# Loading tokens ten blocks ahead in smaller transfers, weights last, and a running maximum in four tiles: a gated long convolution with a soft mixture of experts

## The chip, the core and the metric

The program runs on one core of one Trainium2 chip. The metric is the device time of one execution in microseconds (us), lower is better. A core has a matrix engine (PE, with its weight loads shown apart as PEld), a vector engine (DVE), a scalar engine (ACT), GpSimd (POOL) and SyncE (SP), which here only issues transfers. Sixteen DMA engines carry all transfers.

## What is computed

Two stages follow each other. The first is a long convolution done with FFTs and gated by its input; the second is a soft mixture of experts over the 45,824 tokens of 128 features that come out of it.

```python
u = x * v                                   # batch 4, sequence 11456, 128 features
y = irfft(rfft(u, 2*S) * rfft(filter, 2*S))[:S]
x = (x * y).reshape(45824, 128)

logits = x @ phi                            # 32 slots = 8 experts x 4
d = softmax(logits, over tokens)            # dispatch
slot_input = d.T @ x
h = relu(slot_input[e] @ w1[e])             # 128 -> 1024, for each of 8 experts e
slot_out[e] = h @ w2[e]                     # 1024 -> 128
c = softmax(logits, over the 32 slots)      # combine
out = c @ slot_out
```

All arithmetic is float32.

## The kernel before

**Convolution.** It runs over eight groups of 16 features. A group's last step (`p4`) gives, for seven row blocks in the order 1, 2, 3, 4, 5, 6, 0, a tile of tokens that is gated (`p4_gate`, `last_gate`) and written to a scratch buffer `scr` in device memory (`p4_out`, L465; the remainder by `p4_rest`, L471). `scr` holds x with the 128 features as rows. The last group can only be written at the very end, so its 16 rows (`CG`) of x are the last to come.

**Mixture of experts.** The tokens are cut into 23 blocks of 16 x 128 tokens (the last has 6 x 128), 1 MB each, and two blocks make a unit. Each block is read back from `scr` by `Moe.load` (L692 to L701): one transfer for each part of `scr` that the block touches, up to 2048 tokens long. There are ten places for blocks: five in `ahead_buf` (the tile `ffw`, which is free early) and five in `xbuf` (four in the tile `xreg`, one in the tile `E`). Blocks 0 to 4 go to `ahead_buf`; their first 112 rows (features of groups 0 to 6) are loaded while the last group still computes (`weights`, L655), and their last 16 rows later, by `ahead(t)` (L722), which runs behind each of the seven row blocks t of the last group. Blocks 5 to 9 are loaded whole by `ahead`.

For each unit m the loop of `_moe` does, on PE in this order: `turn` of the unit's first block (32 transposes of 64 x 64, L714), `logits` of the next unit (L780), `turn` of the second block, `dispatch` of the unit before (64 products, L872, four tiles of 32 columns side by side), and `running_max` (L820): one full 128 x 128 product that spreads the row maxima to all partitions, read by a reduction on DVE (L821). The exponentials on ACT (L831) wait for that reduction, and the next unit's logits need the PSUM bank that those exponentials read. Each of these products is issued twice by the hardware's float32 scheme, so a `dispatch` is 64 MATMUL rows and a `running_max` two.

Behind the turn of block i, `fetch(i)` (L952) refills the place that has come free: blocks 10 to 19 behind turns 0 to 9; the eight w1 matrices, two behind each of turns 10 to 13 (`load_w1`, into `ffw`); three w2 matrices behind turn 14; blocks 20 to 22 behind turns 15 to 17; the other five w2 matrices behind turns 18 to 20. One of the three w2 matrices has a place of its own in `ffw`, and the scheduler issues it early. After the last unit come the experts (`up`, `turn_hidden`, `down`) and then the output stage (`spread`, L1128 and L1136), in which 23 MB are written.

**Order of the transfers.** SP issues all of them in program order and stops at one that has to wait. The framework gives them eight completion semaphores in turn, so a transfer also waits until the one eight places before it has landed: at most eight are under way.

Of the kernel before, what the change touches and what calls it, by code (L numbers as in the profile page):

```python
# [29 lines left out]
CG = D // G  # L30
# [33 lines left out]
def conv_part(ctx, tc, cp, moe, xf, vf, xi, xe, pos, w1, w2, win, t1x, t1h, wt, t3, t4, hs, scr):  # L64
# [418 lines left out]
    for g in range(G + 1):  # L483
# [50 lines left out]
        else:  # L534
# [9 lines left out]
            for u in range(NU):  # L544
                p3(g - 1, u)
            moe.places()
            moe.steps = _moe(moe)
            next(moe.steps)

# [89 lines left out]
class Moe:  # L639
# [4 lines left out]
    OB = 4  # L644
    CB = 8 * NB

    def __init__(self, tc, cp, scr, phi, mw1, mw2, rep, out):
# [4 lines left out]
        self.xt, self.xq = {}, {}  # L652
        self.pieces = sorted(_pieces().values())

    def weights(self):  # L655
        nc = self.tc.nc
        w = self.cp.tile([128, 11 * FF], F32, tag="W", name="ffw")
        self.w1t = w[:, : 8 * FF].rearrange("p (e f) -> p e f", e=NEXP)
        self.w2t = {e: w[:, (8 + e) * FF : (9 + e) * FF].rearrange("p (j d) -> p j d", d=128)
                    for e in range(3)}  # L660
# [9 lines left out]
    def load_w1(self, e):  # L670
        self.tc.nc.sync.dma_start(out=self.w1t[:, e], in_=self.mw1[e])

    def load_w2(self, e):
        self.tc.nc.sync.dma_start(out=self.w2t[e],
                                  in_=self.mw2[e])

# [15 lines left out]
    def load(self, i, d0=0, d1=D):  # L692
        q0, n = self.blocks[i]
        t = (self.ahead_buf if i // self.XB in (0, 2) else self.xbuf)[i % self.XB][:, : 128 * n]
        z0, z1 = 128 * q0, 128 * (q0 + n)
        for a, m in self.pieces:
            lo, hi = max(z0, a), min(z1, a + B * m)
            if lo < hi:
                src = self.scr[D * a : D * (a + B * m)].rearrange("(d t) -> d t", d=D)
                self.tc.nc.sync.dma_start(out=t[d0:d1, lo - z0 : hi - z0], in_=src[d0:d1, lo - a : hi - a])  # L700
        self.xt[i] = t.rearrange("p (q t) -> p q t", t=128)  # L701
# [20 lines left out]
    def ahead(self, t):  # L722

        if t == 0:
            make_identity(self.tc.nc, self.ident)
            self.tc.keep_in_program_order(self.tc.nc.vector.tensor_reduce(
                out=self.mask, in_=self.ident.rearrange("p (a s) -> p a s", a=4), axis=AX.X, op=ALU.add))
        for i in ((), (0, 1), (2, 3, 4, 5), (6, 7), (8,), (9,), ())[t]:
            self.load(i, D - CG if i < self.XB else 0)


def _moe(mo):
# [5 lines left out]
    ident = mo.ident  # L738
    phis, reps, w1t, w2t = mo.phis, mo.reps, mo.w1t, mo.w2t

# [206 lines left out]
    hT = mo.obuf[OB - 1].rearrange("p (e j a s) -> p e j a s", e=2, j=FF // 128, a=4)  # L947
    def load_w2(e, j):
        w2t[e] = mo.xbuf[j % XB].rearrange("p (h j d) -> p h j d", h=2, d=128)[:, (e - 3) % 2]
        mo.load_w2(e)  # L950

    def fetch(i):  # L952
        if i < 2 * XB:
            mo.load(i + 2 * XB)
        elif i < 2 * XB + 4:
            for e in range(2 * (i - 2 * XB), 2 * (i - 2 * XB) + 2):
                mo.load_w1(e)
        elif i < 3 * XB:
            for e in range(3):
                mo.load_w2(e)  # L960
# [106 lines left out]
    def up(eg, hf):  # L1067
        ph = mo.plp.tile([128, 512], F32, tag="pl", name=f"ph_{eg}_{hf}")
        for a in range(4):
            inorder(nc.tensor.matmul(ph[32 * a : 32 * a + 32, :], lhsT=siT,  # L1070
                                     rhs=w1t[:, 4 * eg + a, 512 * hf : 512 * hf + 512],
                                     start=True, stop=True, tile_position=(0, 32 * a)))
# [12 lines left out]
    def down(eg, j0=0, j1=FJ):  # L1085
        for j in range(j0, j1):
            for a in range(4):
                inorder(nc.tensor.matmul(po[32 * a : 32 * a + 32, :], lhsT=hT[:, eg, j, a, :],  # L1088
                                         rhs=w2t[4 * eg + a][:, j, :], start=(eg == 0 and j == 0),
                                         stop=(eg == 1 and j == FJ - 1), tile_position=(0, 32 * a)))  # L1090
# [205 lines left out]
```

## Time and profile before

| | us |
|---|---|
| median of 3 runs (888.67 to 893.65) | 889.1 |
| profiled execution, whole time | 892.43 |
| profiled execution, span from first to last instruction | 890.7 |
| of it convolution, to the first logits | 731.9 |
| of it dispatch, from the first logits to the end of the last dispatch | 731.9 to 816.1 |
| experts | 816.1 to 829.0 |
| output | 829.0 to 890.7 |

Times in the rows below are us from the start of the span. PE's clock is granted in full until the output stage. A DMA share of 1.00 means that all sixteen DMA engines are busy.

### The profile page before, as it was taken

How to read it: one execution, taken by the hardware profiler on the slowest of the kernel's cores; microseconds unless marked ns; L12 is line 12 of the kernel's file. 1: busy time of each engine (PE TensorE's matmuls, PEld its weight loads, DVE VectorE, ACT ScalarE, POOL GpSimd, SP SyncE). 2: the span in 40 equal slices, each digit the busy share in tenths (PEclk: the TensorE clock that was granted, in tenths of full speed). 3: DMA queues.
4: the chain of work that ended last, by engine and by line, in shares of the span. 5: the costliest groups of instructions: out<-in, count | busy, mean ns of one | idle time of the engine just before them, and what ended most of it. 6: DMA issues, size and time to landing. Idle time of an engine off the chain costs nothing. (4 is left out here: it accounts for less than half of the span.)

```text
span 890.7 us, 37282 instructions
## 1 busy us (share of the span) xinstructions
PE 857.9 (96%) x16192; PEld 791.0 (89%) x16192; DVE 714.5 (80%) x1239; ACT 455.1 (51%) x971; POOL 393.1 (44%) x538
## 2 busy tenths in 40 slices
PE   9999999999999999999999999999999999899991
PEld 8998989999999999999999999999999987566540
DVE  5967976799799889988988998899789058786791
ACT  5775558315811851472166128415811637887761
POOL 5003860492088019405910960393078013775750
PEclk9999999999999999999999999999999999999996
DMA  9963684457747754775486376557716979993698
GB/s 323 396 197 117 204 246 153 144 155 254 207 135 207 234 166 128 237 237 172 132 261 202 120 222 214 168 166 247 218 44 173 272 176 374 412 355 121 277 416 365
DMA packets 94386, 197.02 MB, mean 221 GB/s; under 512 B 14329, under 2 KB 55707, under 8 KB 90382
## 3 DMA queue, kind: packets, MB, share of 16 engines
q1 hardware_dynamic: 94046, 194.50, 67.0%
q8 instruction: 128, 2.10, 0.9%
q14 instruction: 36, 0.29, 0.1%
q10 hardware_dynamic: 144, 0.07, 0.0%
q0 software_dynamic: 32, 0.07, 0.0%
HBM read 137.73 MB, written 56.86 MB: 218 GB/s over the span
## 5 line engine op out<-in xcount | busy, mean ns | idle before, releaser
L350 POOL TENSOR_TENSOR T<-m 111x256 f32<-111x256 f32 (+1 forms) x199 | 150.9, 758 | 344.8 <-DVE m L344 344.8
L344 DVE TENSOR_TENSOR m<-p,T 111x1024 f32<-111x1024 f32 (+1 forms) x175 | 200.4, 1205 | 14.4 <-PE p L340 7.6
L360 PE MATMUL p<-tab,T 111*99 111x112 f32 x2048 | 205.4, 260 | 1.4 <-POOL T L351 0.3
L360 PEld LDWEIGHTS p<-tab,T 111*99 111x99 f32 x2048 | 198.8, 170 | 6.5 <-issue 1.6
L340 PE MATMUL p<-T,W 128*64 128x128 f32 (+1 forms) x3168 | 197.3, 276 | 0.4 <-issue 0.3
L425 ACT ACTIVATE vc<-p 128x412 f32<-128x412 f32 (+1 forms) x112 | 51.7, 513 | 266.4 <-PE p L412 227.0
L340 PEld LDWEIGHTS p<-T,W 128*64 128x64 f32 (+1 forms) x3168 | 182.0, 127 | 2.8 <-DVE m L344 0.6
L412 PE MATMUL p<-tab,E 99*64 99x103 f32 (+1 forms) x3584 | 174.0, 252 | 1.6 <-DVE E L373 0.6
L412 PEld LDWEIGHTS p<-tab,E 99*64 99x64 f32 x3584 | 166.2, 136 | 3.8 <-ACT vc L425 0.8
L375 ACT ACTIVATE E<-p 99x448 f32<-99x448 f32 x254 | 131.9, 575 | 63.9 <-PE p L360 57.8
L351 POOL TENSOR_TENSOR T<-m 111x256 f32<-111x256 f32 (+1 forms) x199 | 147.4, 741 | 0.0
L186 ACT ACTIVATE T<-p 128x396 f32<-128x396 f32 x240 | 100.2, 535 | 11.3 <-PE p L174 11.1
L174 PE MATMUL p<-tab1x,x 53*64 53x99 f32 x3648 | 86.7, 246 | 0.2 <-ACT E L224 0.2
L174 PEld LDWEIGHTS p<-tab1x,x 53*64 53x64 f32 x3648 | 79.8, 132 | 4.4 <-ACT E L224 0.4
L443 DVE TENSOR_TENSOR p<-p,vc 128x824 f32<-128x824 f32 (+1 forms) x46 | 47.0, 1022 | 8.9 <-ACT vc L425 8.9
L268 DVE TENSOR_TENSOR x<-x,T 128x448 f32<-128x448 f32 x51 | 31.6, 619 | 21.2 <-DMA x<-in_xf_dram 11.6
L274 DVE TENSOR_TENSOR x<-T 128x224 f32<-128x224 f32 x102 | 39.2, 426 | 1.8
L270 DVE TENSOR_TENSOR T<-x 128x224 f32<-128x224 f32 x102 | 39.2, 426 | 1.7
L224 ACT ACTIVATE E<-fl 111x512 f32<-111x512 f32 (+1 forms) x50 | 26.8, 627 | 21.3 <-PE fl L218 21.3
L451 DVE TENSOR_TENSOR E<-p,E 128x824 f32<-128x824 f32 x36 | 36.6, 1017 | 1.2
L720 ACT ACTIVATE xreg<-pt 128x512 f32<-128x512 f32 (+1 forms) x68 | 35.0, 609 | 1.0 <-PE pt L714 0.9
L344 DVE TENSOR_TENSOR m<-p,E 111x1024 f32<-111x1024 f32 (+1 forms) x25 | 28.7, 1201 | 5.1 <-PE p L340 4.9
(156 smaller groups left out, 972.1 us busy)
## 6 DMA issues: line engine op xcount, KB each, us to landing
x<-in_xf_dram SPq DMA_DIRECT2D x114, 256.0 KB, 4.2
out_dram<-xreg SPq DMA_DIRECT2D x16, 1024.0 KB, 10.6
E<-in_xi_dram SPq DMA_DIRECT2D x37, 412.0 KB, 3.9
T<-in_vf_dram SPq DMA_DIRECT2D x65, 224.0 KB, 5.1
scr<-E SPq DMA_DIRECT2D x67, 206.0 KB, 4.3
T<-hs SPq DMA_DIRECT2D x63, 154.0 KB, 4.5
hs<-E SPq DMA_DIRECT2D x12, 784.0 KB, 4.6
mv<-in_vf_dram SPq DMA_DIRECT2D x42, 224.0 KB, 4.6
```

The costliest lines, as they stand in the source:

```text
L174: inorder(nc.tensor.matmul(ps[h][RP * d : RP * d + RP, i, s, :], lhsT=sd[js, i, s, d, :], rhs=tab1x[js, J * (s + d) : J * (s + d + 1)], st ...
L186: inorder(nc.scalar.activation(dst, src, AF.Copy))
L270: inorder(eng.tensor_tensor(out=vt[:, :, m : m + 2], in0=xr[:, :, 0:2], in1=xr[:, :, 2:4], op=op))
L340: inorder(nc.tensor.matmul(ps[ns, i].rearrange("p b c -> p (b c)"), lhsT=W[:, k0 + i, ns], rhs=Tf[:, :, k0 + i, :], start=True, stop=True, ...
L344: inorder(nc.vector.tensor_mul(m[:, :n].rearrange("p k s e c i -> p k s (e c i)").rearrange("p k s (b c) -> p k s b c", c=CG), ps[:, :n].u ...
L350: inorder(eng.tensor_tensor(out=Ty[:, 0], in0=m[:, :n, 0, 0], in1=m[:, :n, 1, 1], op=ALU.subtract))
L351: inorder(eng.tensor_tensor(out=Ty[:, 1], in0=m[:, :n, 1, 0], in1=m[:, :n, 0, 1], op=ALU.add))
L360: inorder(nc.tensor.matmul(pk[:, i, 2 * s : 2 * s + 2, :].rearrange("p q r -> p (q r)"), lhsT=T[0:N1, s, 2 * k + i, u // 2, :, u % 2], rhs ...
L375: inorder(nc.scalar.activation(dst, src, AF.Copy))
L412: inorder(nc.tensor.matmul(pv[RP * h : RP * h + RP, 2 * k + i, w, j0:], lhsT=E[:J, r, 2 - 2 * w + s, :], rhs=tab4[:, s, o + j0 : o + NJ], ...
L425: inorder(nc.scalar.activation(vc[:, w, :, j0:], pv[:, :, 0, j0:], AF.Copy, scale=2.0 * w - 1.0))
L443: inorder(nc.vector.tensor_tensor(out=pw[:, :, :, j0:], in1=vc[:, :, :, j0:], op=ALU.add, in0=pw[:, 1:2, :, j0:].to_broadcast([128, 2, 4, ...
```

## The change

Four edits.

1. `Moe.load` cuts a transfer of more than 700 tokens (`RUN`) into equal parts of at most 700, unless it loads only the last 16 rows.
2. The first 112 rows of blocks 5, 6, 7 and 8 are loaded early as well: block 5 behind the last `p3` of the last group, blocks 6, 7 and 8 in `ahead(0)`, `ahead(1)`, `ahead(2)`. `ahead` then loads only their last 16 rows. Block 9 is still loaded whole.
3. `fetch(i)` loads block i + 10 for i up to 12, so that all x comes before the weights. The weights follow in one list of 16 matrices (w1, then w2): the first into the spare place at the end of `ffw` behind block 22, then two behind each of turns 13 to 20, into the place of the block just turned. Each matrix is two transfers of 512 columns instead of one of 1024.
4. `running_max` is four products, each of 32 columns of `reps` and into 32 partitions, with the same tile positions as `dispatch`, instead of one product of 128 columns.

```diff
+            moe.load(moe.XB, 0, D - CG)
             moe.steps = _moe(moe)
...
+    def load_weights(self, e, place):
+        src = (self.mw1, self.mw2)[e // NEXP][e % NEXP]
+        for f in range(0, FF, FF // 2):
+            self.tc.nc.sync.dma_start(out=place[:, f : f + FF // 2], in_=src[:, f : f + FF // 2])
+        self.wts.append(place)
...
-            if lo < hi:
-                src = self.scr[D * a : D * (a + B * m)].rearrange("(d t) -> d t", d=D)
-                self.tc.nc.sync.dma_start(out=t[d0:d1, lo - z0 : hi - z0], in_=src[d0:d1, lo - a : hi - a])
+            n = max(0, end - lo)
+            parts = -(-n // self.RUN) if d0 == 0 else min(n, 1)
+            cuts = [lo + n * k // parts for k in range(parts + 1)] if parts else []
+            for y0, y1 in zip(cuts, cuts[1:]):
+                self.tc.nc.sync.dma_start(out=t[d0:d1, y0 - z0 : y1 - z0], in_=src[d0:d1, y0 - a : y1 - a])
...
+        if t < 3:
+            self.load(self.XB + 1 + t, 0, D - CG)
         for i in ((), (0, 1), (2, 3, 4, 5), (6, 7), (8,), (9,), ())[t]:
-            self.load(i, D - CG if i < self.XB else 0)
+            self.load(i, D - CG if i < 2 * self.XB - 1 else 0)
...
-        inorder(nc.tensor.matmul(pm, lhsT=reps, rhs=rd.rearrange("p k a -> p (k a)"), start=True, stop=True))
+        for a in range(4):
+            ss = slice(32 * a, 32 * a + 32)
+            inorder(nc.tensor.matmul(pm[ss], lhsT=reps[:, ss], rhs=rd.rearrange("p k a -> p (k a)"),
+                                     start=True, stop=True, tile_position=(0, 32 * a)))
...
     def fetch(i):
-        if i < 2 * XB:
+        if i + 2 * XB < NBL:
             mo.load(i + 2 * XB)
-        elif i < 2 * XB + 4:
-            for e in range(2 * (i - 2 * XB), 2 * (i - 2 * XB) + 2):
-                mo.load_w1(e)
-        elif i < 3 * XB:
-            for e in range(3):
-                mo.load_w2(e)
-        elif i + XB < NBL:
-            mo.load(i + XB)
+            if i + 2 * XB == NBL - 1:
+                mo.load_weights(0, mo.spare)
         else:
-            for e in range(3 + 2 * (i + XB - NBL), min(NEXP, 5 + 2 * (i + XB - NBL))):
-                load_w2(e, i)
+            place = (mo.xbuf if i // XB % 2 else mo.ahead_buf)[i % XB]
+            for h in range(2):
+                if len(mo.wts) < 2 * NEXP:
+                    mo.load_weights(len(mo.wts), place[:, FF * h : FF * h + FF])
```

What SP issues from the last preloads to the 16 rows of blocks 0 and 1, before (rows are destination, source, and partitions x elements; `xl` is the gated output of a row block, `ffw` and `xreg` hold x, `in_mw` are the weights):

```order
L578 DMA E<-in_xe_dram 128x12
L674 DMA ffw<-in_mw_dram 128x1024
L465 DMA scr<-xl_10644 64x824 x2
L700 DMA ffw<-scr 16x2048
L465 DMA scr<-xl_10645 64x824 x2
L700 DMA ffw<-scr 16x1248
L700 DMA ffw<-scr 16x800
```

The same place after the change:

```order
L702 DMA xreg<-scr 112x682
L702 DMA xreg<-scr 112x683 x2
L579 DMA E<-in_xe_dram 128x12
L702 DMA xreg<-scr 112x448 x2
L702 DMA xreg<-scr 112x576 x2
L702 DMA xreg<-scr 112x682
L465 DMA scr<-xl_10644 64x824 x2
L465 DMA scr<-xl_10645 64x824 x2
L702 DMA xreg<-scr 112x683 x2
L702 DMA ffw<-scr 16x2048
L702 DMA ffw<-scr 16x1248
L702 DMA ffw<-scr 16x800
```

Eight transfers stand ahead of the first write of `scr`, two more between the writes and the 16 rows of block 0, and those 16 rows now stand behind the writes of the second row block too.

What SP issues in the dispatch stage from block 18 or 19 on, before (`E` is the fifth place of `xbuf`):

```order
L700 DMA xreg<-scr 128x2048
L700 DMA E<-scr 128x640
L700 DMA E<-scr 128x1408
L671 DMA ffw<-in_mw_dram 128x1024 x8
L674 DMA ffw<-in_mw_dram 128x1024 x2
L700 DMA xreg<-scr 128x1476
L700 DMA xreg<-scr 128x572
L700 DMA xreg<-scr 128x2048
```

The same place after the change, from block 19 on:

```order
L702 DMA E<-scr 128x640
L702 DMA E<-scr 128x469 x2
L702 DMA E<-scr 128x470
L702 DMA ffw<-scr 128x492 x3
L702 DMA ffw<-scr 128x572
L702 DMA ffw<-scr 128x682
L702 DMA ffw<-scr 128x683 x2
L702 DMA ffw<-scr 128x676
L702 DMA ffw<-scr 128x44
L702 DMA ffw<-scr 128x48
L673 DMA ffw<-in_mw_dram 128x512 x8
L673 DMA xreg<-in_mw_dram 128x512 x16
```

The last three blocks now come ahead of the weights and into `ffw`, and no transfer there is longer than 700 elements a row. On PE the order is the same but for the product of `running_max`, and on DVE, ACT and POOL it is the same.

## Rows read from the trace of the kernel before

**Rows 1.** The page: its first part's head (engines), and the third (instruction queue).

```profile
PE 857.9 (96%) x16192; PEld 791.0 (89%) x16192; DVE 714.5 (80%) x1239; ACT 455.1 (51%) x971; POOL 393.1 (44%) x538
...
q8 instruction: 128, 2.10, 0.9%
```

**Rows 2.** Windows: PE, PEld, DVE, ACT, POOL busy (instructions); PE clock, DMA share, GB/s.

```profile
30.00:46.00 16.00, 15.40 (x210) 15.09 (x208) 15.45 (x42) 11.51 (x22) 0.00 (x0) 1.00 1.04 395
...
750.00:800.00 50.00, 45.94 (x1007) 31.73 (x1006) 41.30 (x76) 43.70 (x96) 36.27 (x39) 1.00 1.00 389
...
832.00:884.00 52.00, 38.95 (x248) 18.29 (x246) 37.01 (x67) 31.70 (x59) 23.76 (x36) 0.92 1.01 417
```

**Rows 3.** Timeline of PE in the dispatch stage: start, us, instruction, idle before it.

```profile
749.13 0.39 PE L820 MATMUL pmt<-rd,aux 128*128 128x8 f32 x2
...
755.79 0.39 PE L820 MATMUL pmt<-rd,aux 128*128 128x8 f32 x2
...
762.95 0.39 PE L820 MATMUL pmt<-rd,aux 128*128 128x8 f32 x2
...
766.43 1.06 PE L780 MATMUL pl<-ffw,aux 128*32 128x512 f32 x8 [0.89 <-ACT xreg L720]
...
772.61 0.58 PE L714 MATMUL pt<-aux,ffw 64*128 64x64 f32 x11 [0.95 <-issue]
...
778.32 0.28 PE L714 MATMUL pt<-aux,ffw 64*128 64x64 f32 x2
779.29 1.15 PE L714 MATMUL pt<-aux,ffw 64*128 64x64 f32 x30 [0.70 <-issue]
...
786.00 0.64 PE L872 MATMUL pa<-E,ev 128*32 128x128 f32 x15 [1.03 <-issue]
786.58 0.39 PE L820 MATMUL pmt<-rd,aux 128*128 128x8 f32 x2
```

**Rows 4.** Waits of PE from 440 to 730: us in total, times, longest.

```profile
PE p L340 <- issue: 0.3, 1, 0.3
```

**Rows 5.** DMA packets of 772.61 to 776.70, then queues of 776.70 to 777.90.

```profile
DMA packets 381, 1.68 MB, mean 411 GB/s; under 512 B 42, under 2 KB 42, under 8 KB 277
...
q1 hardware_dynamic: 118, 0.47, 97.8%
q8 instruction: 1, 0.02, 5.5%
```

**Rows 6.** DMA packets of 440 to 730.

```profile
DMA packets 29191, 55.05 MB, mean 190 GB/s; under 512 B 5014, under 2 KB 17606, under 8 KB 28895
```

**Rows 7.** The eight loads of w1 (L671): issue to landing.

```profile
DMA to landing us min/median/max: 8.7/10.6/11.7
```

**Rows 8.** Timeline of PEld at one running maximum, as rows 3.

```profile
749.13 0.30 PEld L820 LDWEIGHTS pmt<-rd,aux 128*128 128x128 f32 x2 [0.20 <-issue]
...
749.45 1.07 PEld L714 LDWEIGHTS pt<-aux,ffw 64*128 64x128 f32 x32
```

**Rows 9.** Timeline of PEld: a dispatch's weight loads.

```profile
747.25 1.69 PEld L872 LDWEIGHTS pa<-xreg,E 128*32 128x32 f32 x64
```

**Rows 10.** Windows before the dispatch stage, columns as rows 2.

```profile
704.00:708.00 4.00, 4.00 (x44) 4.00 (x43) 0.00 (x0) 2.44 (x5) 0.00 (x0) 1.00 1.00 254
716.00:720.00 4.00, 4.00 (x96) 4.00 (x94) 1.24 (x3) 0.92 (x2) 0.00 (x0) 1.00 0.33 102
```

**Rows 11.** Timeline: SP's issues of t = 0, block 0's 16 rows, block 10; first logits.

```profile
720.96 1.74 SPq L465 DMA_DIRECT2D scr<-xl  x2
723.75 0.33 SPq L700 DMA_DIRECT2D ffw<-scr  x1
...
751.40 6.79 SPq L700 DMA_DIRECT2D ffw<-scr  x8
...
731.91 1.92 PE L780 MATMUL pl<-ffw,aux 128*32 128x512 f32 x16
```

**Rows 12.** Loads of 16 rows (L700, 720 to 727): issue to landing.

```profile
DMA to landing us min/median/max: 3.6/3.8/4.1
```

More of the change, by code (lines that the diff above doesn't have):

```diff
@@ L645 @@
     CB = 8 * NB
+    RUN = 700
     def __init__(self, tc, cp, scr, phi, mw1, mw2, rep, out):
@@ L651, in __init__ @@
         self.blocks = [(q, min(self.NB, QN - q)) for q in range(0, QN, self.NB)]
-        self.xt, self.xq = {}, {}
+        self.xt, self.xq, self.wts = {}, {}, []
         self.pieces = sorted(_pieces().values())
@@ L657, in weights @@
         w = self.cp.tile([128, 11 * FF], F32, tag="W", name="ffw")
-        self.w1t = w[:, : 8 * FF].rearrange("p (e f) -> p e f", e=NEXP)
-        self.w2t = {e: w[:, (8 + e) * FF : (9 + e) * FF].rearrange("p (j d) -> p j d", d=128)
-                    for e in range(3)}
+        self.spare = w[:, 10 * FF :]
         aux = self.cp.tile([128, 3 * J], F32, tag="tab1x", name="aux")
@@ L668, in weights @@
             self.load(i, 0, D - CG)
[L670 to L675, printed above, removed]
+    def load_weights(self, e, place):
[3 more added lines that the diff above has]
+        self.wts.append(place)
     def logit_banks(self):
@@ L693, in load @@
         q0, n = self.blocks[i]
-        t = (self.ahead_buf if i // self.XB in (0, 2) else self.xbuf)[i % self.XB][:, : 128 * n]
+        t = (self.xbuf if i // self.XB % 2 else self.ahead_buf)[i % self.XB][:, : 128 * n]
         z0, z1 = 128 * q0, 128 * (q0 + n)
         for a, m in self.pieces:
-            lo, hi = max(z0, a), min(z1, a + B * m)
-            if lo < hi:
-                src = self.scr[D * a : D * (a + B * m)].rearrange("(d t) -> d t", d=D)
-                self.tc.nc.sync.dma_start(out=t[d0:d1, lo - z0 : hi - z0], in_=src[d0:d1, lo - a : hi - a])
+            lo, end = max(z0, a), min(z1, a + B * m)
+            src = self.scr[D * a : D * (a + B * m)].rearrange("(d t) -> d t", d=D)
+            n = max(0, end - lo)
[3 more added lines that the diff above has]
+                self.tc.nc.sync.dma_start(out=t[d0:d1, y0 - z0 : y1 - z0], in_=src[d0:d1, y0 - a : y1 - a])
         self.xt[i] = t.rearrange("p (q t) -> p q t", t=128)
@@ L738, in _moe @@
     ident = mo.ident
-    phis, reps, w1t, w2t = mo.phis, mo.reps, mo.w1t, mo.w2t
+    phis, reps = mo.phis, mo.reps
     inorder = tc.keep_in_program_order
@@ L1070, in up @@
             inorder(nc.tensor.matmul(ph[32 * a : 32 * a + 32, :], lhsT=siT,
-                                     rhs=w1t[:, 4 * eg + a, 512 * hf : 512 * hf + 512],
+                                     rhs=mo.wts[4 * eg + a][:, 512 * hf : 512 * hf + 512],
                                      start=True, stop=True, tile_position=(0, 32 * a)))
@@ L1088, in down @@
                 inorder(nc.tensor.matmul(po[32 * a : 32 * a + 32, :], lhsT=hT[:, eg, j, a, :],
-                                         rhs=w2t[4 * eg + a][:, j, :], start=(eg == 0 and j == 0),
+                                         rhs=mo.wts[NEXP + 4 * eg + a][:, 128 * j : 128 * j + 128], start=(eg == 0 and j == 0),
                                          stop=(eg == 1 and j == FJ - 1), tile_position=(0, 32 * a)))
@@ L1277 @@
                  t1x=k["t1x"], t1h=k["t1h"], wt=k["wt"], t3=k["t3"], t4=k["t4"],
-                 phi=inputs["moe_phi"], mw1=inputs["moe_w1"], mw2=inputs["moe_w2"].reshape(NEXP, FF // 128, 128, D).transpose(0, 2, 1, 3), rep=k["rep"])
+                 phi=inputs["moe_phi"], mw1=inputs["moe_w1"], mw2=inputs["moe_w2"].reshape(NEXP, FF // 128, 128, D).transpose(0, 2, 1, 3).reshape(NEXP, 128, FF), rep=k["rep"])
     nc = _bacc.Bacc("TRN2", target_bir_lowering=False, num_devices=1)
```

3 lines of the change are left out of this document (removed).

## The prediction

> **What bounds the kernel now.** I read the windows first, to find the stages that the change touches. It touches two: the end of the convolution (690 to 742 us) and the dispatch stage (742 to 816). The output stage behind them is a fixed tail: its windows have the DMA engines full at 417 GB/s [rows 2], and 23 MB at that rate are 56 us of the 60 that remain. So whatever the dispatch stage gains or loses moves the end one for one.
>
> In the dispatch stage the DMA engines are full as well, at 389 GB/s from 750 to 800 [rows 2]. PE shows 45.9 busy of 50. Which of the two sets the pace? PE's timeline answers it. From one running maximum to the next is one unit: 749.13 to 755.79 is 6.66 us, with no idle time on PE [rows 3]. That is the pace of PE alone. From 762.95 to 786.58 three units take 23.63 us, 7.88 each [rows 3]. The loss is 23.63 - 3 x 6.66 = 3.65 us. In this stretch lie four idle times of 0.89, 0.95, 0.70 and 1.03, together 3.57 [rows 3]: they are the loss.
>
> They are odd ones. Two stand inside a turn and one inside a dispatch, between products of one tile that is already there. The profile calls three of them "issue", that is, nothing it shows was waited for; the first it gives to ACT, although ACT's results had been there. Counting PE's rows from 772.61 up to 778.32, six of them, the last that stand ahead of 779.29, gives 127 products; the others stand 127 apart too. 127 products have 127 weight loads. The whole kernel has 16192 of each and 128 packets on the queue "instruction" [rows 1]: 253 instructions a packet. So each idle time stands where one packet of PE's instructions ends, and PE waits for the next packet. The DMA view confirms it: from the end of one such wait (772.61) no instruction packet starts for 4.1 us while 1.68 MB of x go by; one starts within 776.70 to 777.90, and PE goes on at 779.29 [rows 3, 5]. **PE waits for its own program, which queues behind x.** From 440 to 730 PE lost 0.3 us in all to "issue" [rows 4], with 190 GB/s and 60% of the packets under 2 KB [rows 6]; in the dispatch stage 42 of 381 packets are that small [rows 5].
>
> The Trainium skill ("Runtime: NRT & Kernel Launch", Instruction fetch mechanics) has instructions refilled in blocks of 256 by a DMA queue of the engine's own, mostly hidden. The block size agrees with the 253; "mostly hidden" does not hold here, by the 0.70 to 1.03. If it held, these waits would be something else, and edits 1 to 3 would gain nothing: that is the second case below.
>
> **The parts of the change.**
>
> *Smaller transfers (edits 1 and 3).* A packet fetched while a page of 127 products runs has about 6 us at PE's pace. It took 4.1 to start, about 1 for itself and about 1.5 to the first product: 6.7 [rows 3, 5]. It is late by 0.7 to 1.0, so the wait need only fall by a quarter, to about 3. Two things shrink. A transfer of a full block has rows of 8 KB, a w1 matrix 4 KB; now none is above 2.8 KB. And at most eight transfers are under way: eight matrices of 0.52 MB at 389 GB/s [rows 2] take 10.8 us, just what they show from issue to landing (median 10.6) [rows 7]; eight parts of 0.35 MB at 395 GB/s take 7.1 us, eight half matrices 5.3. Bounds: nothing, if the wait depends on full engines alone, and the whole 3.65. The waits with 4 KB rows (0.70, 1.03 after w1 has begun) are no shorter than those with 8 KB, which speaks for nothing; the long stretch of small packets with hardly a wait speaks for the whole. I take 3.6.
>
> Do smaller transfers cost bandwidth? From 30 to 46 us transfers of a quarter MB kept the engines full at 395 GB/s [rows 2], against 417 for output transfers of 1 MB: 5% less. A unit needs 2.1 MB in 6.66 us, 315 GB/s. Blocks come ten ahead, five units or 33 us, so neither rate makes PE wait for x. Cost 0. The Trainium skill ("DMA: Bandwidth & Descriptors", Rules for kernel authors) asks for at least 1 MiB a transfer and speaks against this edit; by the rows its price is those 5%, off the path, and the sum by the rule would only lose the gain above.
>
> *Weights last (edit 3).* The same bytes, and the last matrix still goes out behind turn 20, as before. w1, needed first, goes out behind turns 13 to 16, at least two units ahead of `up`. Cost 0; a matrix that came late would hold PE in `up` or `down`.
>
> *Blocks 5 to 8 early (edit 2).* 112 rows of four blocks are 3.67 MB that no longer fall into the full stretch. They do not save PE anything themselves, since PE never waited there for x; they shorten the time in which the engines are full. Their price is before it. The preloads of 112 rows run at 254 GB/s with the engines full until about 716; then these are at a third [rows 10]. Blocks 5 to 7 are 2.75 MB and take 10.8 us from 716, to 727. The 16 rows of blocks 0 and 1, on which the first logits wait, went out from 723.75 and the logits began at 731.91 without a wait for them [rows 11]. Now they stand behind both row blocks' writes and two preloads, so they go out at about 727 to 728.5, and land some 4 us later [rows 12]: 731 to 732.5. The slack is used up. PE stands in order behind the logits, so each us of lateness is a us at the end. Bounds 0 (the idle engines take it all) and 3 (every transfer in the queue waits for its eighth before it). The same squeeze comes again for blocks 2 and 3 behind block 8. I take +1.0.
>
> Later it helps: block 10, held until 751.40 [rows 11] behind the whole blocks 6 to 8, can start some 6 us sooner. PE does not wait for it; the engines only get less full sooner.
>
> *Running maximum in four tiles (edit 4).* The old product costs PE 0.32 us from its first weight load to the next turn's, plus 0.20 of idle time ahead of it where the array changes from four tiles to one [rows 8]: 0.52. The new one is eight weight loads. At dispatch's pace, 64 in 1.69, they take 0.21 [rows 9], and a change of tiling remains, now ahead of the turn. So 0.41, a gain of 0.1 a unit. Upper bound: the 0.32 go entirely. Lower bound: eight loads at the old product's pace, two in 0.30 [rows 8], 1.2 in all, a loss of 0.7. Dispatch's loads lie side by side, so I take the gain: 9 units between the first and last maximum, -0.9, and I round to -0.8, for ACT and DVE are nearly full in these units too.
>
> Sum: -3.6 + 1.0 - 0.8 = -3.4 on the span of 890.7: 887.3. The profiled execution took 892.43 in all, 1.7 around its span, and is 3.3 above the median of the three runs, 889.1. On the median: **885.7 us**.
>
> **The rivals.**
>
> *Instruction waits stay.* The wait for a packet may follow from full engines, not from the size of what stands ahead. For it: 4 KB waited as long as 8 KB. Against it: rows 4 and 6. Then +1.0 - 0.8: 889.3.
>
> *Everything goes well.* The early loads fit into the idle engines, and the maximum gives 0.25 a unit (-2.2), half way to its upper bound beyond the 0.1: 889.1 - 3.6 - 2.2 = 883.3, give or take 2.
>
> *The first logits come late.* One mechanism, at SP: preloads of 112 rows at 254 GB/s ahead of the first writes of `scr`, and the 16 rows of blocks 0 to 3 behind them. It outweighs the 4.4 us of gain once the logits of units 0 and 1 together start over 4.4 us late. Bounds that reach there: all 3.67 MB ahead of them is 14.4 us from 716, 730.4, plus 4 for the write of `scr` and 4 for the load behind it [rows 12]: 738.4, 6.5 late. Against it: the writes stand ahead of blocks 7 and 8 in the queue. Price: 889.1 + 6.5 - 4.4 = 891.2, or 894.8 if the instruction waits stay too.
>
> **Chances.** Forecast (instruction waits gone, 0 to 2 us lost before): 0.55, on its own 883.5 to 887.5. Waits stay: 0.22. Everything well: 0.10. Late logits: 0.10. Four tiles one behind the other (up to +6): 0.03. For 8 in 10 the range leaves out the lower part of the well case and the upper part of the late one: 881.5 to 891. About 1% (8.9 us) is what a measurement can tell from no change; below 880.2 would need every upper bound at once, 0.05; above 898, 0.05; between, 0.90.
>
> **What the new profile would show.** Right: units of about 6.5 us from 760 on, no "issue" idle of 0.7 or more on PE between 760 and 800, GB/s slightly below 389 with a full DMA share, the running maximum as eight MATMUL rows in 0.2 to 0.3 us, first logits at 732 to 733. Wrong: idle times still 127 products apart (the size does not matter); the first logits at 735 or later with PE waiting on `ffw` (the early loads cost more); a longer gap between dispatch and turn (tiles do not overlap).

## The result, and the profile after

| | before | after |
|---|---|---|
| median of six runs each (us) | 889.2 (888.7 to 893.7) | 897.2 (894.9 to 898.6) |
| profiled execution, whole time | 892.43 | 895.18 |
| its span | 890.7 | 893.4 |

The ratio of the two times is 1.0075 with an interval from 1.0051 to 1.0100: the changed kernel is 6.7 us slower by the ratio and 8.0 by the medians, where 3.4 us less were forecast. The profiled executions stand only 2.75 us apart. That of before was longer than five of its six, that of after the second shortest of its six. So I first ask where the profiled 2.7 us of span come from, and then why the median shows more.

PE's timeline of after, from the last products of the convolution (L412) to the first running maximum of the loop (start, us, instruction, idle before it):

```profile
714.41 12.48 PE L412 MATMUL p<-tab,E 99*64 99x103 f32 x274 [0.56 <-DVE E L373]
...
733.37 1.92 PE L784 MATMUL pl<-ffw,aux 128*32 128x512 f32 x16 [0.90 <-DMA ffw<-scr]
...
738.75 1.22 PE L716 MATMUL pt<-aux,ffw 64*128 64x64 f32 x32
742.40 3.64 PE L784 MATMUL pl<-ffw,aux 128*32 128x512 f32 x16 [2.43 <-ACT pmt L992]
745.97 1.97 PE L716 MATMUL pt<-aux,ffw 64*128 64x64 f32 x32
...
749.17 0.25 PE L826 MATMUL pmt<-rd,aux 128*32 128x8 f32 x8
```

PE waits twice: 0.90 us for the 16 rows of blocks 0 and 1, which the profile names, and 2.43 us ahead of the second logits. There it names ACT's copy into `pmt`, which those products do not read. The loads of 16 rows of blocks 2 to 4 say what it was (their issue, and the time to landing of all in this stretch):

```profile
L702 SPq DMA_DIRECT2D ffw<-scr x5: 418/418/463, 734.5 to 736.4; - x5
...
DMA to landing us min/median/max: 4.8/7.7/7.8
```

The first of them, all 16 rows of block 2, went out at 734.47 and landed 7.8 us later, at 742.3; PE went on at 742.40. In [rows 12] such a load took 3.6 to 4.1 us, and the same five of before took 3.8 to 4.1. And the rows behind this wait are too long: the logits took 3.64 us for 1.92, the turn 1.97 for 1.22. The windows of after show why (the third column from the end is PE's granted clock, then DMA share and GB/s):

```profile
736.00:740.00 4.00, 3.82 (x92) 3.36 (x88) 3.33 (x7) 2.25 (x7) 1.32 (x2) 1.00 1.13 231
740.00:744.00 4.00, 1.60 (x8) 0.44 (x12) 1.38 (x2) 2.02 (x6) 0.78 (x2) 0.69 0.86 167
744.00:748.00 4.00, 4.00 (x45) 2.14 (x37) 3.07 (x6) 0.88 (x2) 0.21 (x1) 0.50 0.97 247
748.00:752.00 4.00, 4.00 (x64) 2.70 (x64) 2.13 (x3) 3.67 (x11) 2.80 (x3) 0.96 0.74 167
```

Behind PE's idle time the granted clock was 0.50, the lower of its two levels (1.2 GHz), through 748, and back near 1.00 after it. So lateness cost twice: the wait, and then 2.8 us of slow PE.

**The sum.** The start of the last group's products differs from execution to execution: the row of L412 behind PE's 0.56 us wait for L373 stands at 714.68 before, at 714.41 after and, in the runs below, from 712.68 to 716.42, ahead of all that the change moves on PE. I count from that row ("mark"). Rows of before:

```profile
714.68 17.30 PE L412 MATMUL p<-tab,E 99*64 99x103 f32 x384 [0.56 <-DVE E L373]
...
742.42 0.32 PE L820 MATMUL pmt<-rd,aux 128*128 128x8 f32 x2
...
806.94 0.39 PE L820 MATMUL pmt<-rd,aux 128*128 128x8 f32 x2
...
816.20 0.38 PE L893 MATMUL pmt<-xreg,aux 128*128 128x1 f32 x2
```

And of after, behind its first maximum at 749.17:

```profile
810.87 0.23 PE L826 MATMUL pmt<-rd,aux 128*32 128x8 f32 x8
...
819.22 0.38 PE L900 MATMUL pmt<-xreg,aux 128*128 128x1 f32 x2
```

Before, the first loop maximum stands 27.74 us behind it, the ninth unit's 64.52 later, the product of the denominator (behind the last dispatch) 9.26 later, and 74.50 remain. After, these are 34.76, 61.70, 8.35 and 74.18. So +7.02 - 2.82 - 0.91 - 0.32 = +2.97, and 0.27 less for the mark: the 2.7 us of span. The +7.02 are 1.73 for the first logits, 2.51 more for the second, and 2.78 from there to the maximum (6.77 us for 3.99).

**Who was ahead in the queue.** SP's issues in after (`xreg<-scr` are the preloads):

```profile
722.15 2.82 SPq L465 DMA_DIRECT2D scr<-xl  x4
725.01 1.76 SPq L702 DMA_DIRECT2D xreg<-scr  x2
728.22 1.23 SPq L702 DMA_DIRECT2D ffw<-scr  x3
...
731.09 1.10 SPq L465 DMA_DIRECT2D scr<-xl  x2
732.23 2.19 SPq L702 DMA_DIRECT2D xreg<-scr  x4
734.47 2.32 SPq L702 DMA_DIRECT2D ffw<-scr  x5
```

The same two steps of before, the gated writes of the third row block and the 16 rows of blocks 2 to 4:

```profile
726.98 2.08 SPq L465 DMA_DIRECT2D scr<-xl  x2
729.10 2.58 SPq L700 DMA_DIRECT2D ffw<-scr  x5
```

Block 0's 16 rows go out 4.5 us later than in [rows 11], the gated writes of the third row block 4.1 us later, and behind them stand four more preloads, those of block 8 (732.23), so that the 16 rows of blocks 2 to 4 go out 5.4 us later. Block 10 goes out at 753.44, 2 us later and not 6 sooner. The engines that [rows 10] show at a third from 716 to 720 are now full, at 245 GB/s:

```profile
716.00:720.00 4.00, 4.00 (x96) 4.00 (x94) 1.38 (x2) 0.92 (x2) 0.00 (x0) 1.00 1.06 245
```

The rest of the dispatch stage of after:

```profile
765.26 0.63 PE L784 MATMUL pl<-xreg,aux 128*32 128x512 f32 x4 [0.51 <-issue]
...
770.03 0.23 PE L826 MATMUL pmt<-rd,aux 128*32 128x8 f32 x8
...
777.26 0.52 PE L879 MATMUL pa<-E,ev 128*32 128x128 f32 x10 [0.85 <-issue]
...
790.82 0.22 PE L826 MATMUL pmt<-rd,aux 128*32 128x8 f32 x8
```

In the nine units PE waits twice for instructions, 1.36 us in all, where before it did so four times, 3.57 us (one of them under the name of ACT). The three units of [rows 3], the fourth to the sixth, ran from 770.03 to 790.82: 20.8 us for 23.6. PE waited for no transfer in the nine units.

### The profile page after: what moved, and what is told of

Same layout as the page of the kernel before. It is cut to its first block, busy times and chain, and to the rows that moved or that the text cites. A ratio compares the mean times of both kernels' runs of the same rounds, so it can differ in the third digit from the quotient of the medians.

```text
span 893.4 us, 37570 instructions
## 1 busy us (share of the span) xinstructions
PE 859.0 (96%) x16264; PEld 793.1 (89%) x16264; DVE 716.0 (80%) x1239; ACT 454.8 (51%) x971; POOL 392.7 (44%) x538
## 5 line engine op out<-in xcount | busy, mean ns | idle before, releaser
L412 PE MATMUL p<-tab,E 99*64 99x103 f32 (+1 forms) x3584 | 174.4, 252 | 2.0 <-ACT T L186 1.0
L412 PEld LDWEIGHTS p<-tab,E 99*64 99x64 f32 x3584 | 166.5, 136 | 4.3 <-issue 2.0
```

Of the source, the lines that this page charges most:

```text
L412: inorder(nc.tensor.matmul(pv[RP * h : RP * h + RP, 2 * k + i, w, j0:], lhsT=E[:J, r, 2 - 2 * w + s, :], rhs=tab4[:, s, o + j0 : o + NJ], ...
```

## The experiments

One theory: the early preloads put bytes ahead of the late 16-row loads. Rivals: the cuts do it, because eight transfers under way then hold less; or a cost that the profile does not show. Lines of diffs marked "before" or "after" say which kernel the edit starts from. The table has every run. Ratios are to the kernel before, timed beside them, with their interval, and where the text below gives a difference in us without saying of what, it is worked out from the ratios; the other columns are worked out from PE's timelines as above (mark to first loop maximum; nine units; last loop maximum to the denominator's product), and GB/s of 748 to 764 from the windows.

| run | ratio | mark to maximum | nine units | end | GB/s |
|---|---|---|---|---|---|
| before, second profile of it | | 27.74, 27.74 | 64.52, 64.17 | 9.26, 8.74 | 370, 347 |
| after | 1.0075 (1.0051 to 1.0100) | 34.76 | 61.70 | 8.35 | 314 |
| r_after, the same again | 1.0060 (1.0042 to 1.0079) | 34.81 | 62.60 | 11.76 | 277 |
| e1 after, no edit 2 | 1.0003 (0.9989 to 1.0018) | 27.83 | 61.58 | 9.34 | 336 |
| e2 edit 2 alone | 1.0091 (1.0069 to 1.0113) | 34.10 | 64.68 | 8.43 | 235 |
| e3 after, uncut | 1.0101 (1.0068 to 1.0134) | 35.40 | 65.45 | 8.68 | 225 |
| e4 edit 4 alone | 1.0003 (0.9988 to 1.0018) | 27.83 | 65.38 | 8.65 | 387 |
| e5 thin preloads | 1.0031 (1.0016 to 1.0046) | 27.83 | 66.69 | 10.08 | 310 |
| e6 after, PE kept at work | 1.0030 (1.0014 to 1.0045) | 31.95 | 60.84 | 9.47 | 301 |
| e7 edits 1 and 3 | 0.9987 (0.9973 to 1.0000) | 27.73 | 61.88 | 9.61 | 327 |
| e8 three early blocks | 1.0008 (0.9989 to 1.0027) | 29.57 | 62.33 | 9.92 | 327 |
| e9 as e7, 350 tokens | 1.0086 (1.0058 to 1.0114) | 27.74 | 69.56 | 9.89 | 250 |
| e10 edit 1 alone | 1.0031 (1.0019 to 1.0044) | 27.74 | 67.40 | 8.43 | 318 |
| e11 order of edit 3 alone | 0.9995 (0.9981 to 1.0008) | 27.73 | 63.91 | 8.44 | 387 |
| e12 edits 1 and 4 | 1.0029 (1.0016 to 1.0041) | 27.83 | 65.54 | 8.84 | 336 |
| e13 as e11, 1024 tokens | 0.9998 (0.9985 to 1.0010) | 27.73 | 63.16 | 8.43 | 355 |

### The early preloads: with and without

e1_no_early takes edit 2 out of the changed kernel:

```diff
-            moe.load(moe.XB, 0, D - CG)
...
-        if t < 3:
-            self.load(self.XB + 1 + t, 0, D - CG)
-            self.load(i, D - CG if i < 2 * self.XB - 1 else 0)
+            self.load(i, D - CG if i < self.XB else 0)
```

> The changed kernel without its second edit: blocks 5 to 8 are loaded whole by ahead, as before; cuts, weights last and four tiles stay. Theory (the early preloads stand ahead of the gated writes and of the last 16 rows, and so make the first two logits late): first loop maximum back at 742.4 us instead of 749.2, dispatch units of about 6.5 us as in the changed kernel, 889.2 - 2.8 - 0.9 = 885.5 us. Rival (the cuts themselves make the logits late, because eight transfers under way hold less): first loop maximum at 746 or later, 893 us or more. Rival (a cost that the profiled execution does not show): first loop maximum at 742.4, yet 890 us or more.

PE's timeline, first and last loop maximum:

```profile
741.18 0.25 PE L823 MATMUL pmt<-rd,aux 128*32 128x8 f32 x8
...
802.76 0.22 PE L823 MATMUL pmt<-rd,aux 128*32 128x8 f32 x8
```

No wait ahead of either logits, and the stage before the loop is back to the time of before (27.83 us from the mark). The units are as quick as in after. By the ratio 5 to 6 us came back, to the time of before, but not to the 885.5 expected: the early preloads are the loss, and something of the gain is missing.

e2_only_early puts edit 2 alone into the kernel before (the diff above with its signs turned).

> The kernel before with the second edit alone: the first 112 rows of blocks 5 to 8 early, uncut, weights and running maximum as before. Theory (preloads make the logits late, whatever their size): first loop maximum at 746 to 749 us, about 893 to 896 us, the waits for instructions in the dispatch stage as before. Rival (the cuts are needed for the harm: uncut, a block takes one to three of the eight places): first loop maximum at 743 at most, 888 to 890 us.

8 us slower by the ratio, more than expected, with transfers that are not cut. The first theory holds, the rival of the cuts falls. PE's timeline and windows show what the profile of after does not: with the engines full of preloads, PE waits for its instructions already in the convolution, and its clock falls there.

```profile
722.68 5.91 PE L412 MATMUL p<-tab,E 99*64 99x103 f32 x127 [0.98 <-issue]
730.24 6.87 PE L412 MATMUL p<-tab,E 99*64 99x104 f32 x110 [1.65 <-issue]
```

```profile
732.00:736.00 4.00, 4.00 (x70) 4.00 (x68) 0.85 (x1) 0.93 (x2) 0.00 (x0) 0.72 0.91 214
```

The two waits stand 127 products apart, as in the dispatch stage. So the path is not quite that of after: here the first logits start 4.9 us late behind these two waits, without a wait for their own load. In after one wait of 0.37 us is left there.

e3_uncut sets `RUN = 2048` in the changed kernel.

> The changed kernel with RUN at 2048, so that blocks and preloads go out uncut as before; preloads of blocks 5 to 8, weights last in halves and four tiles stay. Theory: the logits stay late (first loop maximum 746 to 750 us) and PE waits for instructions again while x is read: 897 to 900 us. Rival (the cuts make the logits late): first loop maximum at 743, 886 to 889 us.

As the theory said: late, and 3.75 us slower over nine units than after. With the early preloads, the cuts were a help in the profile, not the harm; the intervals of the two ratios overlap.

### Bytes or places in the queue

e5_thin is e1_no_early with the preloads back, each of 16 rows (the trace has fourteen of them, as in after, not thirteen):

```diff
+            moe.load(moe.XB, 0, 16)
...
+        if t < 3:
+            self.load(self.XB + 1 + t, 0, 16)
```

> e1_no_early with the preloads of blocks 5 to 8 back in their places and in the same 13 transfers, but of 16 rows each instead of 112, a seventh of the bytes; the blocks are then loaded whole, as in e1_no_early (these first reads are read again, so they are extra work and no part of the result). Theory (the bytes: the engines are full and everything behind the preloads waits for them): second logits without a wait on PE, first loop maximum 27 to 29 us after PE's wait for L373 ends (27.8 in e1_no_early, 34.8 in the changed kernel), total within 1 us of e1_no_early. Rival (the eight places: 13 more transfers in SP's queue make it wait, whatever their size): first loop maximum 31 us or more after it, total 4 us or more above e1_no_early.

For the logits it was the bytes: no wait, 27.83 us. The expectation on the total fell: 2.5 us above e1_no_early. With fourteen more transfers the load of block 10 went out some 4 us later than in e1_no_early (counted from the mark), and the nine units took 66.69. Waits of PE from 742 to 820 (us in total, times, longest):

```profile
PE pa L879 <- issue: 3.7, 3, 1.2
PE pt L716 <- issue: 2.8, 4, 1.1
```

6.5 us of waits for instructions, with every transfer cut. So a cut does not take these waits away by itself; here the engines stayed full to 815. The forecast had the cuts take all of them; that is taken up below.

### The clock

e6_warm is the changed kernel with eight unused products on PE ahead of the second logits:

```diff
+    pas[0] = pp.tile([128, 128], F32, tag="pa", name="pa_0")
+    warm(8)
     logits(1)
```

> The changed kernel with eight products of aux by aux (128x128, 16 MATMUL rows, about 2.3 us) put on PE ahead of the second logits, where it was idle 2.43 us; their results are not used. Theory (the second half of the loss comes from the granted clock, which falls behind that idle time): the second logits still start about 9 us after the first, but take 1.9 instead of 3.6 us, clock 1.00 throughout, the first loop maximum some 2.8 us sooner than in the changed kernel counted from the end of PE's wait for L373 (32 instead of 34.8 us). Rival (the clock falls anyhow or the products delay the logits by as much): 34 us or more.

```profile
738.98 2.05 PE L969 MATMUL pa<-aux 128*128 128x128 f32 x16 [1.48 <-DVE vc L431]
740.96 1.92 PE L784 MATMUL pl<-ffw,aux 128*32 128x512 f32 x16
...
745.05 0.25 PE L826 MATMUL pmt<-rd,aux 128*32 128x8 f32 x8
```

```profile
740.00:744.00 4.00, 4.00 (x59) 2.38 (x57) 1.80 (x4) 0.44 (x1) 0.00 (x0) 1.00 1.03 242
```

The second logits start as late as in after (27.86 us behind the mark, there 27.99), but at the full clock, and the maximum comes at 31.95 instead of 34.76: 2.8 us, as expected. The ratio moved with it, from 1.0060 or 1.0075 to 1.0030. The clock's share of the loss is shown. (In e6 the 16 rows went out 1.5 us sooner against the mark than in after, and the logits follow the eight products at once; so the equal start is the products' doing, and what the run compares is the clock behind it.)

### The changed kernel again

> The changed kernel once more, unchanged, timed beside the same runs of the kernel before as the two kernels below. Theory (the lateness differs between executions, as the gated writes, the preloads and the 16 rows fall differently into the eight places): the first loop maximum 32 to 37 us after the end of PE's wait for L373 (34.8 in the first profile), PE's idle time before the second logits 1 to 5 us, median 5 to 8 us above the kernel before. Rival (a fixed loss elsewhere that no profile showed): 34 to 35.5 us again, and a span 3 us above that of the kernel before with a median 8 us above it.

The lateness is the same to 0.05 us (34.81), so the theory that it differs falls. What differs is the end of the stage. Rows of PE's timeline, then windows:

```profile
743.26 3.31 PE L784 MATMUL pl<-ffw,aux 128*32 128x512 f32 x16 [3.25 <-issue]
...
811.30 0.53 PE L879 MATMUL pa<-xreg,ev 128*32 128x128 f32 x11 [1.02 <-issue]
...
817.29 0.65 PE L716 MATMUL pt<-aux,ffw 64*128 64x64 f32 x15 [1.64 <-issue]
...
819.12 0.90 PE L716 MATMUL pt<-aux,ffw 64*128 64x64 f32 x11 [0.18 <-ACT xreg L722]
```

```profile
816.00:820.00 4.00, 2.52 (x55) 2.14 (x58) 1.62 (x4) 1.71 (x6) 3.84 (x5) 0.84 0.08 25
820.00:824.00 4.00, 4.00 (x82) 3.49 (x82) 1.70 (x7) 1.02 (x3) 0.00 (x0) 0.73 0.02 4
```

Here the weights fill the engines up to the last units; PE waits 1.02 and 1.64 us for instructions, and the clock falls again (the 11 products take 0.90 us, elsewhere 0.58). The end takes 11.76 us, 3.4 more than in the first profile. This execution, the longest of nine, lies 8.1 us above the second profile of before: 7.1 of lateness, 1.6 gained in the units, 3.0 lost at the end, 0.4 gained elsewhere. The wait at 743.26 is now named "issue"; the 16 rows, issued from 734.4, landed 8.3 to 8.8 us later, the first of them at 743.2. So the name of this wait was not to be relied on in either profile.

The kernel before once more, for a second profile:

> The kernel before once more, unchanged, for a second profiled execution. Theory (the waits for instructions in the dispatch stage are much the same in each execution): nine units between the first and the last loop maximum in 64 to 65 us again, and the wait for L373 ends anywhere from 712 to 715 us. Rival (the waits differ between executions by as much as edits 1 and 3 gained): 63 us or less.

64.17 us: the waits of [rows 3] come again, within 0.4 us in all.

### Three early blocks, asked for behind the late loads

e8_behind keeps three early blocks, each written behind the 16-row loads of its step:

```diff
-        if t < 3:
-            self.load(self.XB + 1 + t, 0, D - CG)
...
-            self.load(i, D - CG if i < 2 * self.XB - 1 else 0)
+            self.load(i, D - CG if i < self.XB + 3 else 0)
+        if t < 3:
+            self.load(self.XB + t, 0, D - CG)
```

> The changed kernel with three early blocks instead of four (5, 6, 7), each issued behind the 16-row loads of its step instead of ahead of the gated writes that those wait for. Theory (the loss comes from bytes that stand ahead of the late loads): no wait on PE before the first and second logits, first loop maximum 27.8 to 28.6 us after PE's wait for L373 ends, nine units in 61 to 62 us, median 1 to 3 us under the kernel before. Rival (full engines delay the late loads wherever the preloads stand in the queue): first loop maximum 30 us or more after it, median above the kernel before.

SP did not issue them in that order:

```profile
713.86 5.20 SPq L701 DMA_DIRECT2D xreg<-scr  x8
...
730.01 3.82 SPq L701 DMA_DIRECT2D ffw<-scr  x5
```

The eight are blocks 5 and 6 and the first third of block 7 (by their sizes), the same eight as in after, and they still go out ahead of the first gated write at 720.63. What differs from after is the other six: the four of block 8 are not there, and of block 7's two one went out between the first writes (722.73) and one behind the 16 rows of blocks 2 to 4 (730.01). So this run does not show what preloads behind the late loads do, nor whether their place or their number counts. It parts the loss instead. With the eight ahead of the writes the first logits start 1.73 us late, as in after, and the maximum 1.7 us later than in e1_no_early (1.13 of waits for instructions in the convolution, 0.6 that no row shows as idle); there is no wait ahead of either logits. The other 5.3 us of after's 7.0, the wait ahead of the second logits and the clock behind it, are gone with the change to the other six.

The expected 27.8 to 28.6 us and the gain of 1 to 3 us did not come. The ratio does not tell the run from the kernel before: the harm is gone within its interval, and no gain is left.

### The four edits apart

e4_only_tiles is the kernel before with the four products of `running_max` from the change's diff.

> The kernel before with the fourth edit alone: running_max as four products of 32 columns. Theory: 0.1 us a unit, 0.8 in all, 888.4 us (887.9 to 889.0). Rival (the change of tiling also goes): 0.25 a unit, 887.0 us. Rival (nothing): 889.2 us.

A unit without waits takes 6.46 us instead of 6.66 (6.43 in after and e6), twice the gain I had put down. Yet nine units took 65.38. Waits of PE from 740 to 815:

```profile
PE pt L714 <- issue: 2.4, 3, 1.0
PE pa L875 <- issue: 1.5, 2, 1.0
PE pl L780 <- issue: 1.3, 1, 1.3
```

5.2 us of waits for instructions, against 3.6 before. That a quicker PE came to the end of its instructions sooner and so waited longer fits this, but it is argued and not shown. The ratio does not move.

e7_cuts_weights is e1_no_early with the old running maximum: edits 1 and 3.

> The first and third edit alone: cuts and weights last; blocks 5 to 8 whole and the running maximum as before. Theory (cuts remove waits for instructions; e1_no_early ran the nine units between its first and last loop maximum in 61.6 us instead of 64.5): 62 to 62.5 us here, and a median 2 to 3 us under the kernel before. Rival (the profiled execution of e1_no_early was a lucky one, as its median says, 0.7 us above the kernel before): 63.5 us or more, and a median within 1 us of the kernel before.

The units are what the theory said (61.88). The time is 1.2 us below the kernel before by the ratio, between the two theories, and the interval just reaches no change.

e10_cuts_only puts edit 1 alone into the kernel before (its lines in the change's diff).

> The kernel before with the first edit alone (whole blocks and preloads cut at 700 tokens; order of the weights, blocks 5 to 8 and running maximum as before). Theory (the cuts shorten the waits for instructions in the middle, and weights last move the full engines and the waits to the end of the stage): nine units between the first and last loop maximum in 62 to 63.5 us (64.5 before, 61.9 in e7_cuts_weights), and 8.7 to 9.3 us from the last loop maximum to the den product behind the last dispatch (9.6 in e7_cuts_weights), median 1 to 3 us under the kernel before. Rival (the order of the weights did the work): 64 us or more and a median within 1 us of the kernel before.

A miss with a cause that I had priced at nothing:

```profile
800.19 1.94 PE L783 MATMUL pl<-xreg,aux 128*32 128x512 f32 x8 [2.26 <-DMA xreg<-scr]
802.80 1.94 PE L783 MATMUL pl<-xreg,aux 128*32 128x512 f32 x8 [0.67 <-DMA xreg<-scr]
```

The waits for instructions did shrink, to 1.0 us in all. But the last blocks, behind the w1 matrices in the old order, are late, and PE waits 2.9 us for x. It pays more than the wait: the clock was 0.50 from 800 to 804, the two groups of logits took 1.94 us each for 1.07, and the unit took 11.92 us, 5.3 more than a free one.

Why late is argued from the rates: from 748 to 764 cut transfers move 318 GB/s here, uncut ones 347 to 387 (before, e4, e11). From 760 to 790 the two are close, before first and then e10:

```profile
760.00:790.00 30.00, 26.43 (x583) 18.18 (x578) 23.15 (x44) 25.84 (x56) 21.63 (x27) 1.00 1.02 410
```

```profile
760.00:790.00 30.00, 28.69 (x642) 20.34 (x634) 24.68 (x47) 27.58 (x61) 24.05 (x29) 1.00 1.04 397
```

Together that is about 1.2 MB less than before by 790, some 3 us of transfers at this rate (an estimate from these two stretches).

e11_only_weights is the other half: e1_no_early with `RUN = 2048`, whole matrices and the old running maximum.

> The kernel before with the order of the third edit alone: x ten blocks ahead, then the 16 weight matrices, whole; no cuts. Theory: nine units in 64 to 66 us with waits for instructions as before or more, 9.5 us or more from the last loop maximum to the den product, because the weights now fill the engines to the end: median 0 to 2 us above the kernel before. Rival (order did the work in e7_cuts_weights): 62 to 63 us, median 1 to 2 us below.

No change in the ratio; 63.91 us, much as before, and the end, for which I expected 9.5 us or more, took 8.44. So the order alone gives nothing measurable, the cuts alone lose 2.8 us, and both together lie 1.2 below the kernel before, with an interval that reaches no change. Between e10 and e7 lie 4 us, clear of both intervals: edit 3 is what covers the price of the cuts (its order and its half matrices were not tried apart).

e12_cuts_tiles is e10_cuts_only with edit 4.

> e10_cuts_only with the running maximum in four tiles. Theory (a unit without waits takes 6.44 us instead of 6.66, so nine units gain up to 2 us where no packet of instructions is late): 1 to 2 us under e10_cuts_only. Rival (a quicker PE only reaches the end of its instructions sooner, and waits that much longer, as in e4_only_tiles, where nine units took 65.4 us): within 0.7 us of e10_cuts_only.

The same time as e10_cuts_only, as the rival said. The profile has 4.3 us of waits for instructions in the nine units, where e10_cuts_only has 1.0, and 1.5 us of waits for x, where that has 2.9.

### The size of a transfer

e9_run350 (whole blocks cut at 350 tokens, else e7_cuts_weights) and e13_run1024 (at 1024, else e11_only_weights):

```diff
-            parts = -(-n // self.RUN) if d0 == 0 else min(n, 1)
+            parts = -(-n // (350 if d1 == D else self.RUN)) if d0 == 0 else min(n, 1)
```

> e7_cuts_weights (cuts and weights last alone) with the whole blocks cut at 350 tokens instead of 700. Theory (the wait for an instruction packet falls with the size of what stands ahead of it): nine units between the first and last loop maximum in 60.5 to 61.5 us instead of 61.9, idle 'issue' time on PE between 745 and 806 under 0.5 us. Rival (the size does not matter, or more transfers cost SP time): 62 us or more, issue time 1 us or more.

Waits of PE from 740 to 820:

```profile
PE pl L781 <- DMA scr<-xl: 2.5, 1, 2.5
PE pl L781 <- DMA ffw<-scr: 2.2, 2, 1.5
PE pl L781 <- DMA xreg<-scr: 1.6, 1, 1.6
```

In the nine units only 0.5 us of waits for instructions are left, but x comes at 250 GB/s (293 from 760 to 790), and PE waits 6.3 us under the names of transfers: a miss, 7.7 us slower.

> e11_only_weights (x ten blocks ahead, then whole weight matrices) with the whole blocks cut at 1024 tokens; preloads of 112 rows uncut as before. Theory (shorter transfers shorten the waits for instructions, and at 1024 they hardly cost throughput): nine units between the first and last loop maximum in 62 to 63.5 us (63.9 in e11_only_weights, 61.9 in e7_cuts_weights), 360 GB/s or more from 750 to 760, median 1 to 2 us under the kernel before. Rival (half the cut gives none of the gain): 64 us, median within 0.7 us of the kernel before.

Here the preloads of 112 rows are not cut. The units are at the slow side of the theory (63.16), GB/s just under its 360 (359), and the ratio shows nothing. No version here beats the kernel before by more than its interval; e7_cuts_weights comes nearest.

## Why the prediction was wrong, step by step

- **What bounds the stage: held.** Waits for instructions came again in every profile (in e6 only once, 0.45 us behind the nine units, which took 60.84), in the convolution too once its engines were full (e2, 127 products apart). What follows the denominator's product, experts and output, was a fixed tail (74.0 to 74.6 us in all profiles).
- **Blocks 5 to 8 early, +1.0 with bounds 0 and 3: the step that failed.** It costs 5.1 to 6.4 us by the ratios (e1 against after and r_after) and 7.0 in the profile. I worked out the first logits (732 to 733; they came at 733.4) and wrote that "the same squeeze comes again for blocks 2 and 3", without a price of its own. That second squeeze was the larger, 5.3 of the 7.0: SP's writes and loads each moved back by the one before, the 16-row load itself took 7.8 us instead of 4 among full engines, and PE stood idle 2.4 to 3.3 us. And I took a us of lateness for a us at the end; with the clock's fall it was 7.0 for 4.2 (2.8 of it taken back in e6). The rival "late logits" named the place, and I gave it 1 in 10. Its upper bound was 6.5 us of late logits; they were 4.2 us late, and that 6.5 lies close to the 7.0 at the maximum is luck, for the clock was in no case of mine. Its argument against, that the writes stand ahead of blocks 7 and 8, was wrong in weight: eight of the fourteen preloads stood ahead of the first writes, two more ahead of block 0's 16 rows, and the four of block 8 ahead of those of blocks 2 to 4. "Block 10 some 6 us sooner" was wrong too.
- **Waits for instructions, -3.6: right in kind, too large.** In the middle of the stage edits 1 and 3 took 2.3 to 2.6 us (61.88 against 64.17 and 64.52), and gave part of it back at its end, where the weights now stand: 9.61 against 8.74 and 9.26. By the ratio 1.2, with an interval that reaches no change. e5 and r_after show that small transfers do not stop these waits where the engines stay full.
- **Bandwidth, 0: it held for the change, but not at the head of the stage.** In neither profile of the changed kernel did PE wait for a transfer in the nine units. From 760 to 790, with the engines full, the cut loads moved 373 to 397 GB/s (both profiles of after, e1, e7, e8, e10, e12), for 410 before: 3 to 9% less, about the 5% that I had put. But from 748 to 764 they moved 318 to 336 (e1, e7, e8, e10, e12) for 347 to 387, little above the 315 that a unit needs, and in the old order (e10, e12) PE did wait for x. The stretch that I read [rows 2] could not tell this: its transfers were not of a quarter MB alone, five were of half a MB. I had put the rule of the Trainium skill ("DMA: Bandwidth & Descriptors", Rules for kernel authors), at least 1 MiB a transfer, aside at 5%. These runs agree with its direction: from 760 to 790, 399 to 410 GB/s uncut, 393 at 1024 tokens, those 373 to 397 at 700, 293 at 350.
- **Weights last, 0: right in the sum, for the wrong reason.** It is worth about 4 us where edit 1 stands beside it (e7 against e10, where PE waited for x that stood behind the w1 matrices).
- **Running maximum, -0.8: not found.** The products overlap as forecast (eight rows in 0.22 to 0.25 us) and a free unit gains 0.22, but no gain shows in the time: e4 and e12 are level with their partners, e1 is if anything above e7. Part of it went into waits for the exponentials (`et`): 1.1 to 1.3 us in the nine units with four tiles (after, r_after, e1, e4, e12), 0.5 before and 0.5 to 0.8 in the others with the old product.

What stays open: by what the time of an instruction packet goes. Full engines and long transfers both went with longer waits, and no run here moves one without the other. Where the packets end among the products may count too: e6 differs from after by eight products on PE, and its nine units had none of these waits. Open too is why the median of after lies 2 us above its first profile; the late end of r_after would do it, but two profiles do not show that it is the usual one. And open is why e1's median lies above its profile by 3 us; its profile was the fastest of its ten runs.

## What to carry to other kernels

Idle transfer capacity just ahead of a chain of short, late transfers is not free: price every link of that chain, not its first, and read in the trace where the early loads went, for that need not be where the program has them (e8). Cutting transfers shortened the waits behind them in some runs (e7, e9, e10) and not in others (e5, r_after), and it lowers the rate; it needs an order that has the slack for it. And one profile of each kernel can stand several us away from the medians, so a sum of single us needs a second one.

## What the runs showed of the hardware

- A wait of PE is paid twice when the clock falls behind it: after 2.43 us idle the granted clock was 0.50 (1.2 GHz) from 744 to 748, and 2.8 us were lost; with products in the gap it stayed at 1.00 (e6). It does not fall behind every wait: in e12 it was 1.00 from 788 to 804, around a wait of 1.65 us.
- With the engines full of preloads, PE waits for its instructions in the convolution as well, up to 1.65 us in e2 and 2.19 in e3, and the clock fell to 0.72 and 0.71 there.
- A load of 16 rows took 3.6 to 4.1 us from issue to landing in before, and 7.7 to 8.8 us among full engines (blocks 2 and 3 in after and r_after).
- The same instructions ahead of the change start the last group's products at 712.7 to 716.4, from one execution to the next.
